# One transfer made to wait for a small write, and a table load moved to the head of ScalarE's queue

## Chip, core and metric

The kernel runs on one core of a Trainium2 chip. The metric is the device time of one execution in microseconds (us). Times are medians of several runs; the profile comes from one more, separately profiled, execution.

## What is computed

One input x of 2048 rows (time steps) by 512 columns is layer-normalised, and the normalised rows feed two branches whose results are added to x:

```python
xn = (x - mean(x)) / sqrt(var(x) + 1e-5)            # per row
A  = 2 * real(scan(xn @ B_bar.T) @ C.T) + xn * Dskip  # a diagonal complex recurrence over the 2048 rows
B  = (silu(xn @ w_gate) * (xn @ w_up)) @ w_down     # F = 1376 hidden columns
out = x + A + B
```

Inputs and output are bf16. The recurrence multiplies the state by a constant per channel and adds the new row; the kernel turns it into real scans by rotating with cosine and sine tables.

## The kernel before, in words

The 2048 rows are 16 tiles of 128 rows, called x tiles 0 to 15 here; four of them are a chunk of 512 (four chunks). TensorE runs, per chunk, the gate and up products (line 421), the products with B (line 346), the down product (line 501) and the product with C (line 510). ScalarE moves results out of PSUM and applies silu, VectorE (DVE) does statistics, rotations and scans, GpSimd (POOL) a few powers and the accumulating stores.

The order on each engine is written out by hand (`manual_schedule`): instructions go to an engine in the order in which the program names them. The scheduler only adds the semaphore waits. Transfers are issued from SyncE's queue (SP), ScalarE's queue (ACT) and POOL's queue, each in its own order. The transfers issued from SP and ACT signal their landing on eight semaphores that are dealt out in turn, so that the ninth transfer waits until the first user of its semaphore has landed, and so on.

The change is in the head, the first 8 us, in which chunk 0 gets going one x tile at a time:

- Lines 115 to 122 issue eight transfers in turns. SP: x tile 0 (line 115), the first group of gate weights wg0 (line 117), x tile 2 (line 119), the second group wg1 (line 121). ACT: x tile 1 (line 116), the first group of up weights wu0, x tile 3 (line 120), wu1. An x tile has 128 KB, a weight group of these has 256 KB. Line 112 is the helper that issues the weights. Then SP goes on with x tiles 4 to 7 in one transfer of 512 KB (line 126), the larger weight groups, and the transposing loads of B (line 131).
- Lines 153 and 155 are two small DVE writes of constants (-0.5, and the 1e-5 that the layer norm adds), and POOL makes an identity matrix.
- Line 596 loads ScalarE's table for logarithm and exponential, behind ScalarE's four transfers. Line 597 runs 11 dummy matmuls of 512 columns that only keep TensorE busy.
- Lines 598 to 622 then normalise x tiles 0 to 3: statistics on DVE (`ln_stats`, line 174; line 600 for x tile 1, lines 606 and 609 for the halves of x tile 2, line 619 for x tile 3), 1/sqrt by a logarithm and an exponential on ScalarE for x tile 0 (lines 179 and 180) and by a power on POOL for the others (line 184), the normalisation on DVE (line 192), four transposes on TensorE (line 209) with copies back (line 218).
- Line 592 (`head_mm`) is the first useful product: gate and up columns of x tiles 0 to 3 against the first weight groups, as far as tiles and weights are there.

DVE takes these in the program's order: statistics of x tile 0, statistics of x tile 1, normalisation of x tile 0, the rest of x tile 1's statistics, the first half of x tile 2's, normalisation of x tile 1.

```python
    nc.scalar.preload_act_table_set("natural_log_exp_and_others")
    dummy(11, CW)
    ln_stats(0)
    rstd_act(0)
    nc.vector.bn_stats(out=stats[:, 1, :], in_=xall[:, 1, :])
    norm_dve(0)
    nc.vector.bn_aggr(out=mv[:, 1, :], in_=stats[:, 1, :])
    ln_rstd(1, 2)
    xT_pe(0)
    dummy(6, 128)
```

Of the kernel before, what the change touches and what calls it, by code (L numbers as in the profile page):

```python
# [10 lines left out]
F32 = mybir.dt.float32  # L11
# [12 lines left out]
def kernel(  # L24
# [17 lines left out]
    nc = tc.nc  # L42
    _, L, D = A_x.shape
# [3 lines left out]
    CW = 512  # L47
# [3 lines left out]
    TPC = CW // 128  # L51
# [10 lines left out]
    EPS = 1e-5  # L62

    const = ctx.enter_context(tc.tile_pool(name="const", bufs=1))
# [20 lines left out]
    xall = const.tile([128, NT, D], BF16, name="xall")  # L85
# [24 lines left out]
    def load_w1(q, tiles, view, gi):  # L110
        a, b = fgroups[gi]
        q.dma_start(out=tiles[gi][:], in_=view[:, :, a * 128:min(F, b * 128)])


    nc.sync.dma_start(out=xall[:, 0, :], in_=x_v[:, 0, :])
    nc.scalar.dma_start(out=xall[:, 1, :], in_=x_v[:, 1, :])
    load_w1(nc.sync, wg_g, wg_v, 0)
    load_w1(nc.scalar, wu_g, wu_v, 0)
# [30 lines left out]


    ones = nc.const_aps.tensor(1.0, (128, CW), BF16)
    neg_half = const.tile([128, TPC], F32, name="neg_half")
    nc.vector.memset(neg_half[:], -0.5)
    eps_t = const.tile([128, 1], F32, name="eps_t")
    nc.vector.memset(eps_t[:], EPS)
    ident = const.tile([128, 128], BF16, name="ident")
    make_identity(nc, ident[:])
    jidx = const.tile([128, CW], F32, name="jidx")
# [14 lines left out]
    def ln_stats(n):  # L173
        nc.vector.bn_stats(out=stats[:, n, :], in_=xall[:, n, :])  # L174
        nc.vector.bn_aggr(out=mv[:, n, :], in_=stats[:, n, :])  # L175
# [391 lines left out]
    def dummy(n, cols):  # L567
        for _ in range(n):
            nc.tensor.matmul(warm[:, 0:cols], lhsT=ones[:, 0:128], rhs=ones[:, 0:cols], start=True, stop=True)  # L569
# [23 lines left out]
                                 rhs=xnT[:, k, lo * 128:hi * 128], start=(k == 0), stop=(k == KD - 1))  # L593

    allk = range(KD)
    nc.scalar.preload_act_table_set("natural_log_exp_and_others")
    dummy(11, CW)
    ln_stats(0)
    rstd_act(0)
    nc.vector.bn_stats(out=stats[:, 1, :], in_=xall[:, 1, :])  # L600
# [170 lines left out]
```

## Time and profile before

| | us |
|---|---|
| median of 3 runs | 180.82 (180.65 to 181.29) |
| the profiled execution's own time | 180.69 |
| span of its instructions, first to last | 178.9 |
| x tile 0: issued at / landed after | 0.74 / 2.9 |
| x tile 1: issued at / landed after | 0.74 / 3.1 |
| wg0, wu0: issued at / landed after | 1.20 / 4.1, 1.18 / 4.5 |
| x tile 2, x tile 3: issued at / landed after | 1.66 / 4.3, 1.67 / 5.0 |
| wg1, wu1: issued at / landed after | 2.20 / 5.9, 2.29 / 6.0 |
| x tiles 4 to 7: issued at / landed after | 3.86 / 5.9 |
| first transpose of x tile 0 on TensorE | 5.64 |

All times of events count from the span's start. The granted clock of TensorE is 1.000 over the whole span. "Landed after" counts from the start of the issue to the semaphore that says that the data is there. In the profile PE is TensorE's matmul row, PEld its weight loads, DVE VectorE, ACT ScalarE, POOL GpSimd, SP SyncE; ACTq and SPq are the queues' issuing instructions, which count as no engine's busy time. L116 is line 116 of the kernel before. In a line of the timeline, the numbers at its head are the start and the length (from the first start to the last end where several instructions are merged, which the x and a number at its end tell), and brackets give the idle time before it and what ended it.

### The profile page before, as it was taken

Reading aid. Unit: us, or ns where it says so; the run is one execution under the profiler, and the core shown is the slowest. Engines: PE = TensorE matmul, PEld = TensorE weight load, DVE = VectorE, ACT = ScalarE, POOL = GpSimd, SP = SyncE. Lnnn points to the kernel's source line nnn. Section 1 sums busy time; section 2 is a strip of 40 time slices with the busy share of each in tenths; the row PEclk is TensorE's granted clock in tenths of the full one; section 3 lists DMA queues with packets and bytes.
Section 4 is the critical chain, followed back from the end, with each engine's and each line's share of the span. In section 5 each row is a group of like instructions: output and inputs, shape, how many; then the busy total and the mean of one; then the engine's idle time right before and its main releaser. Section 6 shows DMA issues by size and latency. Waiting matters only on the chain.

```text
span 178.9 us, 2451 instructions
## 1 busy us (share of the span) xinstructions
PE 173.6 (97%) x904; PEld 83.5 (47%) x920; DVE 153.4 (86%) x234; ACT 93.8 (52%) x170; POOL 24.9 (14%) x32
## 2 busy tenths in 40 slices
PE   8899999999999999999999999999999999999993
PEld 3684444443444444444444444444444444444743
DVE  1879997999999999999999999999999999950033
ACT  2469876988399957022998661014866610230000
POOL 5223000000500000027200000013405000150000
DMA  6999557994138400021930000007295900073012
GB/s 158 316 288 217 104 107 198 346 182 93 26 64 234 179 0 0 0 20 15 132 72 2 0 0 4 0 0 67 33 135 73 166 2 0 0 79 38 4 47 70
DMA packets 29515, 15.53 MB, mean 87 GB/s; under 512 B 18336, under 2 KB 29440, under 8 KB 29472
## 3 DMA queue, kind: packets, MB, share of 16 engines
q1 hardware_dynamic: 24416, 11.21, 26.4%
q0 software_dynamic: 3456, 3.28, 14.4%
q10 hardware_dynamic: 1632, 0.89, 1.7%
q8 instruction: 7, 0.11, 0.3%
q14 instruction: 4, 0.03, 0.1%
HBM read 8.03 MB, written 5.24 MB: 74 GB/s over the span
## 4 chain that ended last, share of the span: by engine, by line
PE 95%; DMA 2%; DVE 1%; issue 1%
PE ps L421 36%; PE ps L501 21%; PE ps L346 15%; PE ps L510 15%; PE ps L592 3%; PE ps L447 2%; DMA xall<-in_A_x_dram 2%; PE ps L457 1%; PE ps L209 1%; DVE stats L174 0%; DVE stats L600 0%; DVE xall L192 0%; PE ps L569 0%; DVE res L513 0%; DVE mv L175 0%
## 5 line engine op out<-in xcount | busy, mean ns | idle before, releaser
L501 PE MATMUL ps<-wd_sb,guT 128*128 128x512 bf16 (+4 forms) x195 | 38.6, 355 | 0.2
L421 PE MATMUL ps<-xnT,wg 128*128 128x512 bf16 x143 | 37.6, 379 | 0.3
L421 PE MATMUL ps<-xnT,wu 128*128 128x512 bf16 x146 | 37.6, 379 | 0.1
L388 DVE TENSOR_TENSOR_SCAN g<-r_t,car,u 128x512 bf16<-128x512 f32 x24 | 28.9, 1262 | 0.0
L510 PE MATMUL ps<-CF,wt 128*128 128x512 bf16 (+2 forms) x140 | 28.1, 355 | 0.2
L346 PE MATMUL ps<-xnT,BT 128*128 128x512 bf16 x126 | 28.2, 379 | 0.1
L501 PEld LDWEIGHTS <-guT 128*128 128x128 bf16 (+1 forms) x198 | 18.5, 98 | 19.9
L516 ACT CAST res<-ps 128x512 bf16<-128x512 f32 x12 | 7.0, 585 | 38.3 <-PE ps L510 38.3
L435 ACT ACTIVATE guT<-ps 128x512 bf16<-128x512 f32 x40 | 24.8, 619 | 3.6 <-PE ps L421 3.4
L436 ACT CAST u<-ps 128x512 bf16<-128x512 f32 x40 | 24.2, 606 | 4.0 <-PE ps L421 4.0
L517 POOL DMA_DIRECT2D out_dram<-res x12 | 11.1, 999 | 86.9 <-ACT res L516 86.9
L421 PEld LDWEIGHTS <-wu 128*128 128x128 bf16 x148 | 14.5, 98 | 17.5
L421 PEld LDWEIGHTS <-wg 128*128 128x128 bf16 x148 | 14.3, 98 | 17.6 <-issue 0.8
L510 PEld LDWEIGHTS <-wt 128*128 128x128 bf16 x144 | 13.4, 98 | 14.3
L346 PEld LDWEIGHTS <-BT 128*128 128x128 bf16 x128 | 12.5, 98 | 15.1
L348 ACT CAST u<-ps 128x512 bf16<-128x512 f32 x32 | 17.5, 590 | 2.9 <-PE ps L346 2.8
L513 DVE TENSOR_TENSOR res<-ps,xn_end 128x512 bf16<-128x512 f32 (+2 forms) x6 | 3.0, 514 | 14.4 <-PE ps L510 14.4
L440 DVE TENSOR_TENSOR guT<-guT,u 128x1024 bf16<-128x1024 bf16 x20 | 13.5, 680 | 0.0
L184 POOL TENSOR_TENSOR rstd<-ve,neg_half 128x1 f32<-128x1 f32 (+1 forms) x6 | 6.9, 1155 | 40.2 <-DVE ve L183 40.2
L174 DVE BATCH_NORM_STATS2 stats<-xall 128x6 f32<-128x512 bf16 x13 | 8.7, 669 | 2.8 <-DMA xall<-in_A_x_dram 2.8
L356 DVE TENSOR_TENSOR pm<-u,c 128x2048 bf16<-128x2048 bf16 x8 | 9.8, 1220 | 1.2 <-ACT c L273 1.1
L356 DVE TENSOR_TENSOR pm<-g,c 128x2048 bf16<-128x2048 bf16 x8 | 9.7, 1217 | 0.1
(105 smaller groups left out, 158.2 us busy)
## 6 DMA issues: line engine op xcount, KB each, us to landing
out_dram<-in_A_x_dram SPq DMA_DIRECT2D x1, 1536.0 KB, 7.9
out_dram<-res POOLq DMA_DIRECT2D x12, 128.0 KB, 3.1
out_dram<-xall POOLq DMA_DIRECT2D x3, 512.0 KB, 5.9
wd_sb<-in_B_w_down_dram SPq DMA_DIRECT2D x1, 1280.0 KB, 10.1
xall<-in_A_x_dram SPq DMA_DIRECT2D x1, 1024.0 KB, 6.4
wg<-in_B_w_gate_dram SPq DMA_DIRECT2D x2, 384.0 KB, 5.4
wu<-in_B_w_up_dram SPq DMA_DIRECT2D x2, 384.0 KB, 5.6
wu<-in_B_w_up_dram ACTq DMA_DIRECT2D x2, 256.0 KB, 5.2
```

Of the source, the lines that this page charges most:

```text
L174: nc.vector.bn_stats(out=stats[:, n, :], in_=xall[:, n, :])
L346: nc.tensor.matmul(ps[:], lhsT=BT[:, part, k, q * 128:(q + 1) * 128], rhs=xnT[:, k, c * CW:(c + 1) * CW], start=(k == 0), stop=(k == KD - 1))
L348: nc.scalar.copy(out=u_tiles[c][:, part, q, :], in_=ps[:])
L356: V.tensor_tensor(out=t[:], in0=flat(src()[:, i]), in1=flat(tab[:]), op=ALU.mult)
L388: V.tensor_tensor_scan(out=g()[:, part, q, :], data0=r_t[:, q:q + 1].to_broadcast([128, CW]), data1=u_tiles[c][:, part, q, :], initial=ini ...
L421: nc.tensor.matmul(ps[:fs, lo:hi], lhsT=wslice(groups, fi, k), rhs=xnT[:, k, c * CW + lo:c * CW + hi], start=(k == 0), stop=(k == KD - 1))
L435: nc.scalar.activation(out=guT[:fs, fi, :], in_=psg[:fs], func=ACT.Silu)
L436: nc.scalar.copy(out=u_pair[c][:fs, fi % 2, :], in_=psu[:fs])
L440: products.append(lambda: V.tensor_tensor(out=g, in0=g, in1=u, op=ALU.mult))
L501: nc.tensor.matmul(o[:], lhsT=gu_tiles[c][:fsz[fi], fi, i * 128:(i + 1) * 128], rhs=wd_sb[:fsz[fi], fi, lo:hi], start=(fi == 0), stop=False)
L510: nc.tensor.matmul(o[:], lhsT=w_tiles[c][:, part, q, i * 128:(i + 1) * 128], rhs=CF[:, part, q, lo:hi], start=False, stop=(part == 1 and q ...
L517: nc.gpsimd.dma_start(out=out_v[:, n, lo:hi], in_=res[:, lo:hi], accum_op=ALU.add)
```

## The change

Three edits, all in the head. The two DVE writes of constants and ScalarE's first table load come before all transfers in the program. A new DVE write of zeros to the first 256 columns of x tile 1's place stands between the issue of x tile 0 and that of x tile 1; x tile 1's transfer writes to the same place, so it must wait for that DVE write, and what follows on ACT's queue stands behind it. One of the 11 dummy matmuls goes.

```diff
+    neg_half = const.tile([128, TPC], F32, name="neg_half")
+    nc.vector.memset(neg_half[:], -0.5)
+    eps_t = const.tile([128, 1], F32, name="eps_t")
+    nc.vector.memset(eps_t[:], EPS)
+
+    nc.scalar.preload_act_table_set("natural_log_exp_and_others")
+
     nc.sync.dma_start(out=xall[:, 0, :], in_=x_v[:, 0, :])
+    nc.vector.memset(xall[:, 1, 0:D // 2], 0.0)
     nc.scalar.dma_start(out=xall[:, 1, :], in_=x_v[:, 1, :])
...
-    neg_half = const.tile([128, TPC], F32, name="neg_half")
-    nc.vector.memset(neg_half[:], -0.5)
-    eps_t = const.tile([128, 1], F32, name="eps_t")
-    nc.vector.memset(eps_t[:], EPS)
...
-    nc.scalar.preload_act_table_set("natural_log_exp_and_others")
-    dummy(11, CW)
+    dummy(10, CW)
```

In the program that is built from it, ACT's order becomes: table load, x tile 1 (waits for DVE), wu0, x tile 3, wu1, and then the logarithm. The eight landing semaphores are dealt out in another order, which moves two waits: the transfer of x tiles 4 to 7 on SP, which waited for x tile 1 to land, waits for nothing now; and wu1 on ACT, which waited for nothing, now waits until x tile 0 has landed. The waits of SP's later transfers fall on other early transfers. On PE one dummy matmul and its weight load are missing; on POOL nothing changes; on DVE the new write stands third. Everything else keeps its place.

## The prediction

> **What bounds the kernel now.** I read the page's busy shares first, then the table by stretches of time, then the chain that ended last, then the head in the timeline, and last the transfers' times to landing.
>
> ```profile
> PE 173.6 (97%) x904; PEld 83.5 (47%) x920; DVE 153.4 (86%) x234; ACT 93.8 (52%) x170; POOL 24.9 (14%) x32
> ```
> ```profile
> 1.75:2.45 0.70, 0.70 (x4) 0.16 (x2) 0.00 (x0) 0.00 (x0) 0.70 (x2) 1.00 0.88 56
> 2.45:3.25 0.80, 0.80 (x3) 0.28 (x2) 0.00 (x0) 0.47 (x1) 0.79 (x3) 1.00 1.06 337
> ...
> 8.05:20.00 11.95, 11.90 (x110) 7.90 (x110) 10.47 (x32) 9.19 (x20) 3.06 (x4) 1.00 1.08 240
> 20.00:170.00 150.00, 149.21 (x709) 68.65 (x722) 135.84 (x183) 81.45 (x143) 18.78 (x18) 1.00 0.37 69
> ```
>
> TensorE bounds it. In each row the first pair is PE's busy time: from 8.05 on PE has 11.90 of 11.95 us and then 149.21 of 150 us. So the end moves as PE's start of useful work moves, if nothing becomes late on the way, and only the head can give something. The last two numbers are the DMA engines' busy share and GB/s: when x tile 0 begins to flow, the engines are 0.88 busy but move 56 GB/s; only from 2.45 on do they move 337.
>
> ```profile
> 0.74 2.90 DMA xall<-in_A_x_dram
> 3.67 0.71 DVE stats L174
> 4.39 0.18 DVE mv L175
> 4.58 0.59 DVE stats L600
> 5.17 0.42 DVE xall L192
> ```
> ```profile
> 0.74 0.41 ACTq L116 DMA_DIRECT2D xall<-in_A_x_dram  x1
> 0.74 0.40 SPq L115 DMA_DIRECT2D xall<-in_A_x_dram  x1
> ...
> 2.78 1.28 ACT L596 ACT_TABLE_LOAD   x1 [2.78 <-issue]
> ...
> 4.61 0.29 ACT L179 ACTIVATE ve<-mv,eps_t 128x1 f32<-128x1 f32 x1 [0.55 <-DVE mv L175]
> 4.94 0.20 ACT L180 ACTIVATE rstd<-ve 128x1 f32<-128x1 f32 x1
> 5.17 0.41 DVE L192 TENSOR_SCALAR xall<-xall,mv,rstd 128x512 bf16<-128x512 bf16 x1
> ...
> 5.64 0.40 PE L209 MATMUL ps<-ident,xall 128*128 128x128 bf16 x4 [0.81 <-DVE xall L192]
> ...
> 5.97 0.43 DVE L606 BATCH_NORM_STATS2 stats<-xall 128x6 f32<-128x256 bf16 x1
> ...
> 6.56 0.60 DVE L192 TENSOR_SCALAR xall<-xall,mv,rstd 128x256 bf16<-128x256 bf16 x2 [0.16 <-POOL rstd L184]
> ```
> ```profile
> xall<-in_A_x_dram ACTq DMA_DIRECT2D x1, 128.0 KB, 3.1
> xall<-in_A_x_dram SPq DMA_DIRECT2D x1, 128.0 KB, 2.9
> ```
>
> The chain starts with x tile 0's transfer (landed at 0.74 + 2.90 = 3.64), then its statistics, and then its normalisation at 5.17 has two things to wait for that end together: ScalarE's 1/sqrt (4.94 + 0.20 = 5.14) and, ahead of it on DVE, x tile 1's statistics (4.49 + 0.66 = 5.15). Both are counted from landings: 5.17 is x tile 0's landing plus 1.53, and x tile 1's statistics could have begun at its landing, 0.74 + 3.1 = 3.84, but DVE was free only at 4.49. **x tile 1 has 0.65 us to spare**, x tile 0 none.
>
> **The change, part by part.**
>
> *DVE's write and x tile 1's issue.* The three writes follow the barrier: 0.81, 0.84, so the third at 0.87. A DVE write of 256 columns is in no row. Below stands the DVE write of 4 columns, 0.06 us; above, half of line 192, 128x256 read and written, 0.34. I take 0.2: a write alone, wider than the first and simpler than the second (POOL's 128x128 write took 0.22). DVE is idle until 3.67, so it costs DVE nothing. With 0.04 for the hand-over (as from line 175's end at 4.57 to line 179 at 4.61), x tile 1 is issued at 0.87 + 0.2 + 0.04 = 1.11 (0.97 to 1.25), 0.37 later.
>
> *What x tile 0 gains.* In the trace's packet records x tile 0's packets run from 1.77 to 3.22, x tile 1's from 2.37 to 3.35. Each of the 16 engines has one of x tile 0's first packets stall for 0.25 to 0.69 us (others take 0.046); until 2.37 only 32 of 128 have started. Then both tiles go in turns, and some 120 KB of x tile 1 move before x tile 0 is done. At 337 GB/s these are 0.36 us, the most to be gained. If x tile 1's first packet moves with its issue, to 2.74, x tile 0 has the engines alone for 0.29 us at 337 GB/s, 98 KB, about the 96 it still lacks. The engine that stalls longest is free at 2.71; six packets of 0.046 bring it to 2.99 instead of 3.22: **0.23 us** earlier, bounds 0 and 0.36. x tile 1 then lands at 3.84 + 0.37 = 4.21, and DVE wants it at 4.49 - 0.23 = 4.26: just in time.
>
> *What comes next.* x tile 1's power ended at 6.53 with 0.13 us of cover over the half statistics of x tile 2 (5.97 to 6.40), which began as x tile 2 landed (1.66 + 4.3 = 5.96). If that landing stays, line 192 for x tile 1 gains only 0.13; if the later x tile 1 lets SP's queue ahead, up to 0.23. I take **0.2** for the path. Other landings behind x tile 1 may slip by its 0.37: wu0 5.68 to 6.05 (used at 7.09 - 0.2), x tile 3 6.67 to 7.04 (7.85 - 0.2), wu1 8.29 to 8.66 (9.58 - 0.2); wg1 on SP at 8.10 is used at 8.71 - 0.2. All still hide.
>
> *Table load first.* It runs at 0.74 to 2.02 instead of 2.78 to 4.06; the logarithm waited 0.55 us for DVE, so nothing was lost there and nothing is won, but x tile 0's earlier statistics would leave 0.3. Costed at nothing if ACT can issue a transfer while the table loads; no row shows an issue beside a busy ACT, so the bounds are 0 and the whole 1.28 us on x tile 1 (below). The Trainium skill (Advanced Engine Details and Errata, Sequencer and Instruction Queues) says that engine instructions are pushed to a queue and that the sequencer reads on; by that rule the issue is not held, and the sum stays. No run here shows it yet.
>
> *The two moved waits.* wu1 is issued after x tile 0 lands, about 3.45 to 3.95 instead of 2.29. Its first packet came at 5.57, behind x tile 3's, so 1.6 us of queueing cover it. The logarithm stands behind it on ACT and is wanted at 4.61 - 0.23 = 4.38: 0.4 us to spare. x tiles 4 to 7 go out at about 2.7 instead of 3.86; they stand behind wg1 on SP's queue, whose packets end at 7.48, and are wanted at 12.61, landing at 9.76: nothing. The larger groups behind them start on other landings, within about 1 us of before, and SP's chain has slack to line 346 at 20.06.
>
> *One dummy less.* The eleventh took 0.22 us (spacing 0.43 at first, 0.22 from the eighth on) and PE sat idle 0.81 after it: nothing. Ten at the slow 0.43 would end at 5.1, still before the transposes at 5.44.
>
> **Sum.** -0.2 us on a profiled execution of 180.69 (span 178.9, 1.8 around it), 180.49. That execution lies 0.13 below the median of 180.82, so **180.6**.
>
> **Rivals.**
>
> *Nothing gained, 180.8.* x tile 1's packets came 1.63 us after its issue, x tile 0's only 1.03, and the last stores' 0.84 to 0.89 after theirs. So x tile 1's were perhaps held by something common, the stalled first packets or one maker of descriptors: 1.11 + 1.03 = 2.14 is still before 2.37, the two interleave as now, and x tile 0 gains nothing. For it: the first ACT packets start as the first stalls end, at 2.37 to 2.43. Against it: an engine that began an SP packet at 2.23 did not take an ACT packet, so that one was hardly waiting then. The Trainium skill (DMA: Bandwidth & Descriptors, Queues, rings and completion order) has a rule that comes to the same end: an engine drains a whole packet of some 9 to 17 descriptors from one ring before it turns to another. x tile 0 gives each engine eight packets in the trace's sense and one landing mark; taken first, they would lose nothing to x tile 1. The trace speaks against the rule here: five engines started on ACT's queue by 2.43, when only 32 of x tile 0's 128 had started in all.
>
> *The table load holds x tile 1, 181.5 (the slower side).* If ACT issues nothing while it loads, x tile 1 goes out at 0.74 + 1.28 + 0.03 = 2.05, lands 1.31 later at 5.15, its statistics end at 5.17 + 0.66 = 5.83, and x tile 0's normalisation behind them starts at 5.85 instead of 5.17: +0.68, 181.50. It decides from a landing of 4.49 on. For it: one queue in order, table load before transfer, and before the change all transfers stood ahead of the load. Against it: x tile 1 might flow faster when issued late, beside SP alone.
>
> *wu1 late, 181.2.* If x tiles 4 to 7, released early, go ahead of wu1 (512 KB at 307 GB/s, the row for 5.65 to 8.05, is 1.7 us), wu1 lands at 9.99, PE wants it at 9.38: +0.61 - 0.2. Against it: two queues that shared evenly.
>
> **Chances.** Forecast (0.1 to 0.4 faster) 0.45, nothing gained 0.22, table load 0.22, wu1 late 0.08, something else 0.03. Range 180.2 to 181.5: from the whole 0.36 and a little scatter up to the table load's price. What a measurement here can tell from no change is about 0.3%, 0.54 us. Faster by more than that needs more than the 0.36 that x tile 1 takes from x tile 0: 0.10. Slower by more is most of the table load's case (+0.68) and a little of wu1's and the rest: 0.20. Within: 0.70.
>
> **What the changed profile would show.** x tile 1's issue at 1.0 to 1.25 (near 2.05: the table load holds it). x tile 0's landing at 3.3 to 3.5 (3.64: nothing gained). Line 192's first start near 4.95, PE's first transpose near 5.4, and PE without gaps from about 7.85. If x tile 1's statistics, not ScalarE, release line 192, x tile 1 came too late. The prediction is wrong if PE waits for weights before 10 us, or if the head wins and the time does not.

## The result, and the profile after

The changed kernel takes **181.42 us** (median of 7 runs, 181.21 to 181.59) against 180.82 (7 runs, 180.46 to 181.29): 1.0031 times as long, 95% interval 1.0016 to 1.0045. It is slower by 0.6 us; 0.2 us faster was forecast. The profiled execution took 181.26, its span is 179.5.

The page's busy shares say that TensorE is still the bound and has its 97%, over a span 0.6 us longer:

```profile
PE 174.2 (97%) x919; PEld 83.4 (46%) x919; DVE 153.5 (86%) x235; ACT 93.6 (52%) x170; POOL 24.9 (14%) x32
```

The chain of waits over the first 14 us (start, length, what) names the loss:

```profile
0.74 2.06 DMA xall<-in_A_x_dram
2.80 0.02 issue
2.82 7.29 DMA wu<-in_B_w_up_dram
10.11 0.04 issue
10.16 1.50 PE ps L597 x20
```

x tile 0 now lands at 0.74 + 2.06 = 2.80 instead of 3.64. But the chain goes on through a weight transfer, wu1: issued at 2.82, landed 7.29 later at 10.11, and TensorE starts on it at 10.16. Before, wu1 went out at 2.29, landed at 8.29 and was not in the chain. The timeline of the changed kernel's head:

```profile
0.74 1.28 ACT L120 ACT_TABLE_LOAD   x1 [0.74 <-PEq L759]
...
0.90 0.17 DVE L124 MEMSET xall<- 128x128 uint32 x1
1.09 0.43 ACTq L125 DMA_DIRECT2D xall<-in_A_x_dram  x1
...
2.68 0.51 SPq L135 DMA_DIRECT2D xall<-in_A_x_dram  x1
2.82 0.39 ACTq L112 DMA_DIRECT2D wu<-in_B_w_up_dram  x1
2.82 0.69 DVE L179 BATCH_NORM_STATS2 stats<-xall 128x6 f32<-128x512 bf16 x1 [1.76 <-DMA xall<-in_A_x_dram]
...
4.33 0.41 DVE L197 TENSOR_SCALAR xall<-xall,mv,rstd 128x512 bf16<-128x512 bf16 x1
...
5.88 0.43 DVE L610 BATCH_NORM_STATS2 stats<-xall 128x6 f32<-128x256 bf16 x1 [0.85 <-DMA xall<-in_A_x_dram]
...
6.22 0.59 DVE L197 TENSOR_SCALAR xall<-xall,mv,rstd 128x256 bf16<-128x256 bf16 x2
...
10.15 0.33 PEld L597 LDWEIGHTS <-wu 128*128 128x128 bf16 x4 [0.96 <-DMA wu<-in_B_w_up_dram]
10.16 0.61 PE L597 MATMUL ps<-xnT,wu 128*128 128x256 bf16 x4 [0.87 <-DMA wu<-in_B_w_up_dram]
```

Lines 120, 124, 125, 135, 179, 197, 597 and 610 are lines 596, new, 116, 126, 174, 192, 592 and 606 of the kernel before. Read from the top: the table load runs over x tile 1's issue and does not hold it (1.09, inside 0.74 to 2.02). **x tiles 4 to 7 leave SP at 2.68 with no wait shown, 1.18 us earlier than before and 0.14 ahead of wu1.** That is the two moved waits at work: x tiles 4 to 7 lost theirs, wu1 got one, on x tile 0's landing. Normalisation of x tile 0 starts 0.84 us earlier (4.33 for 5.17), that of x tile 1 only 0.34 (6.22 for 6.56), because DVE then waits 0.85 us for x tile 2. At 10.15 the weight load has been idle 0.96 us for wu1. The last matmul starts at 176.46 instead of 175.87: +0.59, the whole loss.

Two of TensorE's rows split it: the gate product just ahead of wu1's, and wu1's. Before:

```profile
8.71 0.60 PE L592 MATMUL ps<-xnT,wg 128*128 128x256 bf16 x4
9.58 0.61 PE L592 MATMUL ps<-xnT,wu 128*128 128x256 bf16 x4
```

In the changed kernel the first comes 0.36 earlier, the second (10.16 above) 0.58 later, so wu1 costs 0.94:

```profile
8.35 0.60 PE L597 MATMUL ps<-xnT,wg 128*128 128x256 bf16 x4
```

The transfers from 6 to 7 us, first before, then in the changed kernel (queue q1 is SP's, with the end of wg1 and with x tiles 4 to 7; q10 is ScalarE's, with wu1; packets, MB moved):

```profile
q10 hardware_dynamic: 301, 0.15, 54.7%
q1 hardware_dynamic: 306, 0.15, 53.9%
```
```profile
q1 hardware_dynamic: 432, 0.27, 101.8%
q10 hardware_dynamic: 13, 0.01, 2.1%
```

And between 7 and 9 us in the changed kernel:

```profile
q1 hardware_dynamic: 495, 0.47, 69.0%
q10 hardware_dynamic: 471, 0.24, 39.3%
```

Up to 7 us SP's queue has the engines almost alone. In the trace's packet records x tiles 4 to 7 start to flow at 6.24 and wu1 at 6.56; before, it was 6.98 and 5.57. From 7 to 9 the two queues moved about as many packets, but SP's carried twice the bytes: a row of x is 1024 bytes, a row of wu1 512. So wu1 starts late and then flows slowly. The even count of packets is no rule: e9 shows another.

### The profile page after: what moved, and what is told of

It is laid out like the page before. It is cut to its first block, busy times and chain, and to the rows that moved or that the text cites. A ratio compares the mean times of both kernels' runs of the same rounds, so it can differ in the third digit from the quotient of the medians.

```text
span 179.5 us, 2466 instructions
## 1 busy us (share of the span) xinstructions
PE 174.2 (97%) x919; PEld 83.4 (46%) x919; DVE 153.5 (86%) x235; ACT 93.6 (52%) x170; POOL 24.9 (14%) x32
## 3 DMA queue, kind: packets, MB, share of 16 engines
HBM read 8.03 MB, written 5.24 MB: 74 GB/s over the span
## 4 chain that ended last, share of the span: by engine, by line
PE 93%; DMA 5%; DVE 0%; issue 0%
PE ps L426 36%; PE ps L506 21%; PE ps L515 15%; PE ps L351 15%; DMA wu<-in_B_w_up_dram 4%; PE ps L452 2%; PE ps L597 2%; DMA xall<-in_A_x_dram 1%; PE ps L462 1%; DVE res L518 0%; PE ps L214 0%
## 5 line engine op out<-in xcount | busy, mean ns | idle before, releaser
L506 PE MATMUL ps<-wd_sb,guT 128*128 128x512 bf16 (+3 forms) x198 | 38.8, 356 | 0.0
```

What stands on the lines that cost most here:

```text
L506: nc.tensor.matmul(o[:], lhsT=gu_tiles[c][:fsz[fi], fi, i * 128:(i + 1) * 128], rhs=wd_sb[:fsz[fi], fi, lo:hi], start=(fi == 0), stop=False)
```

## The experiments

Two theories of the loss. **A**: x tiles 4 to 7, released early, take the DMA engines from wu1. **B**: ScalarE's queue is late, and wu1 with it, whatever SP does. "Tail" is the span's end minus the last matmul's start; times are medians, ratios are to the kernel before measured beside each (180.82 for the changed kernel, 180.60 or 180.66 for the experiments), with their 95% intervals.

| run | time | ratio | x tile 0 landed | wu1 issued / landed | x tiles 4 to 7 issued | last matmul | tail |
|---|---|---|---|---|---|---|---|
| before | 180.82 | 1 | 3.64 | 2.29 / 8.29 | 3.86 | 175.87 | 3.05 |
| changed | 181.42 | 1.0031 [1.0016, 1.0045] | 2.80 | 2.82 / 10.11 | 2.68 | 176.46 | 3.03 |
| e1_hold47 | 180.81 | 1.0015 [1.0006, 1.0023] | 2.99 | 2.60 / 8.57 | 3.98 | 175.34 | 3.53 |
| e2_table_first | 181.82 | 1.0065 [1.0052, 1.0077] | 3.36 | 3.38 / 10.35 | 2.68 | 176.69 | 3.05 |
| e3_wait_only | 180.72 | 1.0004 [0.9996, 1.0013] | 2.94 | 2.60 / 9.42 | 2.96 | 175.76 | 3.03 |
| e5_hold47_wu1late | 180.94 | 1.0022 [1.0012, 1.0032] | 2.96 | 2.95 / 8.03 | 3.94 | 175.23 | 3.52 |
| e6_hold_one_wait | 180.42 | 0.9983 [0.9972, 0.9994] | 3.05 | 3.08 / 8.67 | 3.82 | 175.36 | 3.04 |
| e7_hold_x2first | 181.02 | 1.0018 [1.0002, 1.0034] | 2.90 | 2.92 / 8.73 | 3.67 | 175.85 | 3.06 |
| e8_before_two_waits | 181.15 | 1.0029 [1.0018, 1.0041] | 3.48 | 2.29 / 8.36 | 3.72 | 175.78 | 3.52 |
| e9_halves (one run) | 181.11 | – | 3.00 | 3.02 / 9.01 | 2.68 | 175.35 | 3.99 |
| e10_other_two_waits | 181.12 | 1.0021 [1.0012, 1.0031] | 3.66 | 2.29 / 8.6 | 3.90 | 175.89 | 3.53 |
| e11_three_waits | 181.01 | 1.0020 [1.0011, 1.0028] | 3.59 | 2.29 / 8.4 | 3.88 | 175.92 | 3.36 |

Landings, last matmul and tail come from one profiled execution of each kernel. In some it took clearly less than the median (0.42 us in e5, 0.32 in e7, 0.31 in e2, 0.21 in e6, 0.13 in e1), and no trace shows what the longer executions lost.

**e1: x tiles 4 to 7 held until x tile 0's statistics.** All of SP's later transfers of the head (x tiles 4 to 7 first) move into a function that is called behind them:

```diff
+    def load_more():
+        nc.sync.dma_start(out=xall[:, TPC:2 * TPC, :], in_=x_v[:, TPC:2 * TPC, :])
...
     ln_stats(0)
+    nc.vector.memset(xall[:, TPC, 0:2], 0.0)
+    load_more()
```

> The changed kernel, but x tiles 4 to 7 are issued only after a small DVE write to their place that stands behind x tile 0's statistics (about 3.75 instead of 2.68 us); with that wu1's wait for x tile 0 falls away too (issue about 2.55 instead of 2.82). Theory A (x tiles 4 to 7, released early, go ahead of wu1 and make it late): wu1 lands near 8.7 instead of 10.11, PE does not wait for it near 9.2, and the head's gain comes through: about 0.35 us under the kernel before, 180.4 to 180.5. Rival B (wu1 and all of ScalarE's queue are late because x tile 1's wait and wu1's own wait delay them; the big transfer does not matter): wu1 lands at 9.7 or later, PE still waits 0.5 us or more, 181.1 to 181.4.

PE's wait is gone: in the table by stretches, PE (first pair) is busy in all of the 0.96 us of which it was busy for 0.09 in the changed kernel. First the changed kernel, then e1:

```profile
9.20:10.16 0.96, 0.09 (x2) 0.01 (x1) 0.56 (x2) 0.55 (x2) 0.89 (x2) 1.00 1.11 325
```
```profile
9.20:10.16 0.96, 0.96 (x16) 0.93 (x15) 0.70 (x2) 0.38 (x2) 0.72 (x2) 1.00 1.10 339
```

The last matmul starts at 175.34, 1.12 us earlier than in the changed kernel and 0.53 earlier than before. That speaks for A. Of SP's later transfers only x tiles 4 to 7 are really held: the third gate group goes out at 4.55 (4.73 in the changed kernel). But the time did not follow: 180.81, no better than before. In the profiled execution the tail behind the last matmul, which grew from 3.05 to 3.53, takes the gain back. That was unexpected and became a question of its own (e6, e8, e10, e11).

**e2: table load first, without the DVE write.**

```diff
-    nc.vector.memset(xall[:, 1, 0:D//2], 0.0)
```

> The changed kernel without the DVE write to x tile 1's place: x tile 1 is issued beside x tile 0 at 0.74, the table load first, one dummy less, and both moved waits stay (x tiles 4 to 7 without a wait, wu1 behind x tile 0's landing). If the 0.34 us by which the write delays x tile 1 is what lets x tile 0 land at 2.80, x tile 0 lands near 3.6 again with stalled first packets. Theory A: wu1 is then issued near 3.65, well behind x tiles 4 to 7, lands at 10.2 to 10.8, PE waits 0.6 to 1.2 us for it, 181.4 to 182.0. Rival B: wu1 is late only by its own later issue, 0.5 to 1.3 us of which the queue hides most, 180.8 to 181.2. If the table load were what speeds x tile 0, it would still land near 2.8.

Slower still: x tile 0 lands at 3.36, wu1 goes out when it has landed, 0.70 behind x tiles 4 to 7 instead of 0.14, and lands at 10.35. So 0.56 of the 0.84 gained at x tile 0 hangs on the write's delay; the table load alone does not bring it.

**e3: the write, with the table load back in its old place.**

```diff
-    nc.scalar.preload_act_table_set("natural_log_exp_and_others")
     nc.sync.dma_start(out=xall[:, 0, :], in_=x_v[:, 0, :])
...
+    nc.scalar.preload_act_table_set("natural_log_exp_and_others")
     dummy(10, CW)
```

> The changed kernel with the table load back behind ScalarE's four transfers. In the program that comes out of it x tile 1 still waits for the DVE write, but wu1 waits for nothing and x tiles 4 to 7 wait for x tile 0's landing (about 2.82 instead of 2.68, behind wu1 at about 2.5). x tile 0 should still land near 2.8. The table load would run to about 4.2, so the logarithm and with it line 192 for x tile 0 come about 0.45 later than in the changed kernel (4.8 instead of 4.33), which x tile 2's late landing hides: x tile 1's normalisation stays near 6.2. Theory A (order of the two issues): wu1 lands near 8.5 to 9.0, no wait of PE for it, 180.4 to 180.6. Rival B (delay of ScalarE's queue): wu1 near 9.5 or later, 181 or more.

No difference that can be measured. The timeline shows what the moved load is worth once x tile 0 is early:

```profile
3.09 1.28 ACT L598 ACT_TABLE_LOAD   x1 [3.09 <-issue]
4.38 0.29 ACT L181 ACTIVATE ve<-mv,eps_t 128x1 f32<-128x1 f32 x1
4.71 0.20 ACT L182 ACTIVATE rstd<-ve 128x1 f32<-128x1 f32 x1
4.94 0.41 DVE L194 TENSOR_SCALAR xall<-xall,mv,rstd 128x512 bf16<-128x512 bf16 x1 [0.49 <-ACT rstd L182]
```

The load ends at 4.37 and the logarithm follows at once at 4.38; x tile 0's normalisation gains 0.23 instead of 0.84. wu1 again shares with x tiles 4 to 7, though it was issued 0.36 ahead of them: its 9.42 lies above what A expected (8.5 to 9.0) and just under what B did (9.5), so e3 does not decide between them.

**e5: e1, with wu1 made later still** by three DVE writes to its place, the wait that B blames:

```diff
+    for _ in range(3):
+        nc.vector.memset(wu_g[1][:], 0.0)
     load_w1(nc.scalar, wu_g, wu_v, 1)
```

> As e1_hold47, but wu1 waits for three DVE writes over its whole place, so that it is issued at about 2.8 to 2.9, as late as in the changed kernel, while x tiles 4 to 7 are still held to about 3.8. It tells wu1's late issue from the early big transfer. Theory A: as e1_hold47, wu1 near 8.7 and 180.4 to 180.6. Rival B: wu1 near 9.7 or later and 181 or more.

wu1 is issued at 2.95, later than in the changed kernel, and lands at 8.03, two microseconds earlier. B falls: with x tiles 4 to 7 out of the way the late issue costs nothing. The tail is again 3.52.

**e6: e1, with one wait less on SP.** The write and the call stand between the two statistics instructions of x tile 0, so that x tiles 4 to 7 wait for DVE alone and wu1 keeps the landing of x tile 0 as its wait:

```diff
-    ln_stats(0)
+    nc.vector.bn_stats(out=stats[:, 0, :], in_=xall[:, 0, :])
+    nc.vector.memset(xall[:, TPC, 0:2], 0.0)
+    load_more()
+    nc.vector.bn_aggr(out=mv[:, 0, :], in_=stats[:, 0, :])
```

> As e1_hold47, but the small DVE write that holds x tiles 4 to 7 stands directly behind x tile 0's statistics (issue near 3.6), and in the program that comes out SP's transfer then has one wait instead of two, while wu1 keeps its wait for x tile 0's landing (issue near 2.85). In e1_hold47 TensorE's last matmul came 0.53 us earlier than before, but SP's last steps took about 0.45 longer; its instruction stream has one wait more. Theory A with that tail cost: wu1 lands near 8.5 although it is issued as late as in the changed kernel, PE does not wait, TensorE ends near 175.35, and with no tail cost the time is 0.4 to 0.55 us under the kernel before. Rival B (wu1's own wait): PE waits near 9.2, 0.3 us or more over the kernel before. If the tail cost has nothing to do with SP's count of instructions, the time is again that of e1_hold47, about 0.2 over before.

Same head as e1 (last matmul 175.36), old tail (3.04): **180.42, ahead of both kernels**, 0.17% under the kernel before. In the profiled execution the span is 0.5 us shorter than before (178.4 for 178.9); in the medians 0.18 us of it is left. wu1 was issued at 3.08, later still than in e5, and landed at 8.67, so B falls here too.

**e7: e6, with x tile 2 ahead of wg0 on SP**, since DVE's order waited for x tile 2:

```diff
+    nc.sync.dma_start(out=xall[:, 2, :], in_=x_v[:, 2, :])
     load_w1(nc.sync, wg_g, wg_v, 0)
...
-    nc.sync.dma_start(out=xall[:, 2, :], in_=x_v[:, 2, :])
```

> As e6_hold_one_wait, and SP issues x tile 2 ahead of wg0. It tests what ate half of x tile 0's gain: in the changed kernel x tile 0's normalisation starts 0.84 earlier, x tile 1's only 0.34, as the statistics of x tile 2 stand ahead of it on DVE and wait for a landing at 5.85. With x tile 2 landing near 4 the normalisation of x tile 1 should start near 5.75, the first use of wu0 then waits for its landing (near 5.7), and TensorE should end 0.2 to 0.4 earlier than in e6: 0.6 to 0.9 us under the kernel before. If wg0, now behind x tile 2, lands after 5.5 and PE waits for it instead, the gain over e6 is lost.

The wait only moves, and the 0.6 to 0.9 us hoped for do not come. wg0 is now behind, and the timeline shows PE waiting for it:

```profile
6.50 0.62 PE L598 MATMUL ps<-xnT,wg 128*128 128x128 bf16 x8 [0.33 <-DMA wg<-in_B_w_gate_dram]
```

Last matmul and tail are those of the kernel before (175.85, 3.06); the 0.18% in the medians the trace does not explain.

**e8: the kernel before, with a double wait for x tiles 4 to 7**, to measure the tail by itself:

```diff
+    nc.vector.memset(xall[:, TPC, 0:2], 0.0)
     nc.sync.dma_start(out=xall[:, TPC:2 * TPC, :], in_=x_v[:, TPC:2 * TPC, :])
```

> The kernel before with nothing but one more thing to wait for: a tiny DVE write to x tiles 4 to 7's place near 0.8 us, long done when their transfer is issued at 3.86. The head stays as it is (first transpose near 5.64, last matmul near 175.87); SP's instruction stream has one wait more. If that is what costs e1_hold47 and e5_hold47_wu1late 0.45 at the end: 0.3 to 0.5 us over the kernel before, with the gap before SP's last drain near 0.45 instead of 0.05. If the tail cost comes from something else: within 0.1 us of before.

The last matmul starts 0.09 earlier than before, the time is 0.29% longer: the tail alone. The write makes x tiles 4 to 7 wait for two things, and a second wait is an instruction of its own: SP has 83 instructions in the trace instead of 82.

**e9: the changed kernel, with x tiles 4 to 7 in two transfers of half the columns**, 512-byte rows like wu1's:

```diff
-    nc.sync.dma_start(out=xall[:, TPC:2 * TPC, :], in_=x_v[:, TPC:2 * TPC, :])
+    for lo in (0, D // 2):
+        nc.sync.dma_start(out=xall[:, TPC:2 * TPC, lo:lo + D // 2], in_=x_v[:, TPC:2 * TPC, lo:lo + D // 2])
```

> The changed kernel with x tiles 4 to 7 fetched as two transfers of half the columns (rows of 512 B instead of 1024 B; the second half waits for wg0's landing). In the changed kernel between 7 and 9 us the two queues moved 495 and 471 packets, but 0.47 and 0.24 MB, so they take turns by packets and the queue with larger packets gets more. If so, wu1 shares evenly with the first half, its bytes move in about 1.7 instead of 3 us, and it lands near 8.8 to 9.3 instead of 10.11, though x tiles 4 to 7 are still issued ahead of it; PE's wait shrinks to 0 to 0.2. If instead the transfer issued first is served first, wu1 lands at 9.7 or later. SP has one instruction more, so the end may cost 0.45 as in e1_hold47.

wu1 lands at 9.01 instead of 10.11, though the first half goes out at 2.68 as in the changed kernel, and the trace lists no wait of PE for it (its product starts at 9.06). The two queues from 7 to 8 us, first in the changed kernel, then in e9:

```profile
q1 hardware_dynamic: 251, 0.26, 75.3%
q10 hardware_dynamic: 177, 0.09, 29.9%
```
```profile
q10 hardware_dynamic: 376, 0.19, 75.4%
q1 hardware_dynamic: 240, 0.12, 44.8%
```

By the packet records wu1 starts to flow as late as in the changed kernel (6.62 and 6.56), but its last packet starts at 8.36 instead of 9.49. While both queues have work they do not take turns packet by packet: with rows of 512 bytes on both, wu1's queue moves 376 packets to SP's 240, with SP's rows of 1024 it moves 177 to 251. So e9 supports A; how much of the 1.1 us is the shorter rows and how much the division in two it does not separate, and by what rule the queues share stays open. The tail of 3.99 has two parts. SP has 83 instructions here too (below); and with one transfer more, the stores' semaphores are dealt out otherwise, so that SP begins its waits at the end with the store that lands last. From 170 us on SP's waits show it (total, times, longest):

```profile
SPq L771 <- DMA out_dram<-res: 1.1, 1, 1.1
```

Its eight further waits, some 0.06 us each, come behind that one (0.48 in all) instead of beside it.

**e10 and e11: where the tail's half microsecond comes from.** Each is the kernel before. e10 has a DVE write for another transfer, so that SP has 83 instructions and x tiles 4 to 7 keep one wait; e11 has three such writes, 85 instructions:

```diff
+    nc.vector.memset(wg_g[2][:, 0, 0:2], 0.0)
     load_w1(nc.sync, wg_g, wg_v, 2)
```
```diff
+    nc.vector.memset(xall[:, TPC, 0:2], 0.0)
     nc.sync.dma_start(out=xall[:, TPC:2 * TPC, :], in_=x_v[:, TPC:2 * TPC, :])
+    nc.vector.memset(wg_g[2][:, 0, 0:2], 0.0)
     load_w1(nc.sync, wg_g, wg_v, 2)
+    nc.vector.memset(wu_g[2][:, 0, 0:2], 0.0)
     load_w1(nc.sync, wu_g, wu_v, 2)
```

> The kernel before with one small DVE write (128x2) to the place of the third gate-weight group, so that this group's transfer on SP's queue, and not x tiles 4 to 7, waits for two things: SP again has 83 instructions instead of 82, by another transfer. Theory 'the number of SP's instructions decides the tail': the head and the last matmul's start stay as in the kernel before (175.8 to 175.9), the end comes 3.5 us after it instead of 3.05, the page counts 5 packets of instructions on q14 instead of 4, and the time is 0.2 to 0.35% above the kernel before. Rival 'it was the double wait on x tiles 4 to 7 itself': the tail is 3.05, the time within 0.1%.

> The kernel before with three such DVE writes, so that x tiles 4 to 7 and the third gate and up groups each wait for two things: SP has 85 instructions. Theory 'a load of code falls into the end once the program crosses a boundary': the load of code for SP's last instructions begins earlier by the two further instructions, and as SP waits more than 1 us for the last store's landing just ahead of its last instructions, the load is hidden: a tail of 3.05 to 3.1, 5 packets on q14, the time within 0.1% of the kernel before. Rival 'each added SP instruction costs at the end': a tail of 4.0 to 4.5 and 0.5 to 0.8% more. Between them, 'once past the boundary always the same': a tail of 3.5 and 0.25 to 0.3% more.

e10 has e8's tail, 3.53: it is the count of SP's instructions and not the double wait on x tiles 4 to 7. e11's is 3.36, between, so the tail neither grows with each instruction nor hides at 85. The trace tells why. Listed by number, SP stands still for 0.47 to 0.50 us **between its 79th and its 80th instruction in each of the twelve profiles**. In the kernel before this is the wait for itself in SP's waits from 170 us on:

```profile
SPq L766 <- SPq L766: 0.5, 1, 0.5
SPq L766 <- DMA out_dram<-res: 0.4, 1, 0.4
SPq L766 <- PEq L766: 0.2, 1, 0.2
```

With 82 instructions (before, changed, e2, e3, e6, e7) the 80th is a wait in the last exchange between the engines, and POOL clears semaphores meanwhile: in the kernel before SP goes on at 178.60, POOL is done at 178.64. With 83 (e1, e5, e8, e9, e10) it is the instruction before, with which SP reports the stores as landed; all others wait for that, and the pause is on the path whole (in e8 177.96 to 178.43). With 85 (e11) it is the wait for the last store, which lands inside the pause (177.99, in 177.87 to 178.34), so a part is covered. Neither "hidden" nor "each adds" came true, and "always the same" only nearly. What makes SP pause at that number the traces do not show; a load of code, which I had expected, is not shown. The page counts five packets of instructions on q14 for e10, as expected there, and four for the kernel before, but the last of them comes at 179.18, behind the pause (178.08 to 178.55); in the kernel before it comes at 179.44, after the span's end.

## Why the prediction was wrong

- **The step that failed is "The two moved waits".** It costed x tiles 4 to 7 leaving early at "nothing" and gave wu1 "1.6 us of queueing cover". The cover was the order on the DMA engines, and the edit changed that order: x tiles 4 to 7 went out 0.14 us ahead of wu1 and began to flow 0.32 ahead of it, where they had begun 1.41 behind. Measured: wu1 landed 1.82 later, PE's weight load idle 0.96, the last matmul 1.12 later than with x tiles 4 to 7 held (e1). The sign of being wrong that the prediction itself named, PE waiting for weights before 10 us, came. The mechanism stood among the rivals as "wu1 late" at 0.08, with a landing of 9.99 (measured 10.11) and 181.2 (measured 181.42). "Against it: two queues that shared evenly" did not hold: from 6 to 7 us SP's queue moved 432 packets and ScalarE's 13, and from 7 to 9 SP's moved twice the bytes.
- **What x tile 0 gains was mis-sized**: 0.23 forecast, at most 0.36; measured 0.84 in the changed kernel. Where x tile 1 is issued 0.35 us after x tile 0 (changed, e1, e3, e5, e6, e7, e9) x tile 0 landed at 2.80 to 3.05; where both are issued together (before, e2, e8, e10, e11) at 3.36 to 3.66. The bound counted only the bytes that x tile 1 takes and held the stalls of the first packets as they were. These were 0.25 to 0.69 us before; they are at most 0.24 in the changed kernel and 0.30 in e1. They are not all of it: in e2 they are at most 0.34, and x tile 0 still lands at 3.36. What shortens them is not shown. Whether the gain speaks against the Trainium skill's rule (DMA: Bandwidth & Descriptors, Queues, rings and completion order) of whole packets of some 9 to 17 descriptors before an engine turns to another ring, no run here shows: the packet records do not name the engine.
- **What comes through** was forecast as 0.2, limited by x tile 2's landing. The limit is right in kind (DVE idle 0.85 for x tile 2 at 5.88); with wu1 on time the last matmul starts 0.53 (e1) and 0.51 us (e6) earlier than before. Some of that is x tile 2, which lands at 5.68 and 5.70 there for 5.85 in the changed kernel.
- **DVE's write and x tile 1's issue** were right: 0.17 us (0.2 taken), issue at 1.09 (1.11).
- **Table load first** was right in that the load holds no transfer, so the rival of 181.5 falls. The sequencer rule of the Trainium skill (Advanced Engine Details and Errata, Sequencer and Instruction Queues) agrees with the issue at 1.09 beside a load that runs to 2.02. It was wrong in "nothing is won": with the load in its old place x tile 0's normalisation starts 0.61 us later than in the changed kernel (e3), of which 0.14 is x tile 0's landing (2.94 for 2.80).
- **One dummy less** cost nothing: PE was idle ahead of the first transpose in the changed kernel too (0.38 us).

So the +0.59 at the last matmul is, to rounding, -0.36 for the head and +0.94 for wu1; the prediction had -0.2 and 0.

## What to carry to other kernels

A wait put ahead of one transfer shifts all that stand behind it on its queue, and through the shared semaphores may let the other queue go sooner: list the new order of all transfers on the engines, and ask which small one that is needed soon now runs beside a big one. Here the queue that began first had the engines almost alone at first, and the one with the longer rows then got more of the bytes. Hold the big transfer until the small ones are out, and compare the tail as well as the head: one more wait on a queue engine can cost what the head has won.

## What the runs showed of the hardware that was not expected

- Two first transfers of 128 KB on two queues, x tiles 0 and 1: issued together, x tile 0 landed at 3.36 to 3.66 us (five profiles); with x tile 1 issued 0.35 us later, at 2.80 to 3.05 (seven). The means differ by 0.6 us, more than the 0.36 that the prediction worked out for x tile 1's bytes.
- Which of two queues gets more of the DMA engines was not a matter of even turns: from 7 to 8 us SP's queue moved 251 packets of 1024 bytes to ScalarE's 177 of 512 in the changed kernel, and 240 to 376 with 512 bytes on both (e9).
- SP paused 0.47 to 0.50 us at one fixed number of its instructions, behind the 79th, in all twelve profiles. Whether that costs anything depends on which instruction falls there: 0.48 us with 83 instructions (e8, 1.0029 [1.0018, 1.0041]; e10, 1.0021 [1.0012, 1.0031]), 0.31 with 85, next to nothing with 82.
